# Loading the first head's keys as two halves in a long decode-attention kernel

## The chip, the cores and the metric

The kernel runs on one core of a Trainium2 chip. The metric is the device time of one execution in microseconds (us), of the slowest core, which here is the only one. "A 2% change" would be 27 us. A load is issued when SyncE hands it to the DMA queue, and it has landed when the last of its data are in the buffer.

## The reference

Two decode steps with one query token each, side by side. Part A has 32 heads with 32,768 keys each. Part B has 32 query heads on 8 key heads and a window of the last 4,096 keys.

```python
q = x @ wq                                   # 1 x 512 times 512 x 4096, then 32 heads of 128
scores = einsum(q, k_cache) * 128 ** -0.5    # A: 32 heads x 32768 keys; B: the last 4096 keys
p = softmax(scores)
out = einsum(p, v_cache).reshape(1, 4096) @ wo
return concatenate([A, B])
```

Each head of part A has 8 MB of keys and 8 MB of values (the MB of the load list, 2^20 bytes), and each byte is used once.

## The kernel before

Part B runs first, then a loop over the 32 heads of part A. The key buffer has three thirds of 4 MB. A head of A takes two of them, alternately (1, 0) and (1, 2). The value buffer holds one head of A. All loads are issued by SyncE, in order, into one queue; SyncE waits with each load until the buffer that it overwrites has been read.

```python
def load_k(self, g, parts):
    w = HALF * DH
    src = self.kv_src("k", "A", g)[:, 0, :]
    lo = min(self.k_thirds(g))
    free = [self.free["k"][t] for t in self.k_thirds(g)]
    if parts == 1:
        self.load(self.kbuf[:, w * lo:w * lo + 2 * w], src, self.mark("k", 0), *free)
        sem = self.mark("k", 1)
        self.op("sp", lambda e: e.sem_inc(sem, 16))
    else:
        for i, t in enumerate(self.k_thirds(g)):
            self.load(self.kbuf[:, w * t:w * t + w], src[:, w * (t - lo):w * (t - lo) + w], self.mark("k", i), *free)
# ...
for g in range(NQH):                       # NQH = 32
    self.loop = {"pe": g, "dve": g // 2}
    self.load_k(g, 1 if g < NQH - 1 else 2)   # the last head is split already
    self.load_v(g)
    self.emit_qcopy(g)
    self.emit_unit("A", g)     # TensorE transposes the keys (L560), VectorE copies (L564), TensorE: scores (L583)
    self.emit_stats("A", g)    # maximum and exponentials
    self.emit_PT("A", g)       # TensorE transposes the probabilities
    self.emit_PV("A", g)       # TensorE: probabilities times values (L663)
```

TensorE's program is one loop for all heads. It waits for semaphore `ksem0` before a head's first half and for `ksem1` before its second. With a single load, `ksem0` tells of the landing, and SyncE itself raises `ksem1`, so that the loop's waits are the same for both forms.

Of the kernel before, what the change touches and what calls it, by code (L numbers as in the profile page):

```python
# [10 lines left out]
NQH = 32  # L11
# [42 lines left out]
class _Kernel:  # L54
# [118 lines left out]
    def emit(self, eng):  # L173
# [22 lines left out]
        def body(e):  # L196
# [17 lines left out]
            for k, it in enumerate(need):  # L214
                cur, plan = {}, []
                for n in it:
                    w = []
                    for name, (sem, val) in n.items():
                        if name not in sems:
                            continue  # L220
                        rel = val - start[name] - step[name] * k
                        if rel > cur.get(name, 0):
                            cur[name] = rel
                            w.append((name, rel))
                    plan.append(sorted(w))
                plans.append(plan)
            for k, plan in enumerate(plans):
                for p, q in zip(plan, plans[-1]):
                    assert p == q or (k == 0 and set(p) <= set(q)), (eng, k, p, q)
# [126 lines left out]
# [5 lines that stand above are left out]
        if parts == 1:  # L361
            self.load(self.kbuf[:, w * lo:w * lo + 2 * w], src, self.mark("k", 0), *free)
            sem = self.mark("k", 1)
            self.op("sp", lambda e: e.sem_inc(sem, 16))
        else:
            for i, t in enumerate(self.k_thirds(g)):
                self.load(self.kbuf[:, w * t:w * t + w], src[:, w * (t - lo):w * (t - lo) + w], self.mark("k", i), *free)
# [26 lines left out]
    def plan(self):  # L394
        self.lsem = {"k": self.ksem, "v": self.vsem}
        self.fill = {w: [0, 0] for w in "kv"}
        self.free = {"k": [None] * 3, "v": [None] * 2}
        self.nbatch = 0
        self.copies = []
        self.pending = []  # L400
        self.psread = self.ptread = self.sread = self.accread = None
        self.gath = self.qcopy = self.hcopy = self.qread = None
        self.constants()
        a, b = self.X["A"], self.X["B"]

        self.load_wq("B")
        self.load_b("k", 0)
        self.load_wq("A")
        self.load_b("k", 1)
        self.emit_qproj("B")  # L410
        self.emit_unit("B", 0)
        self.emit_qproj("A")
        self.emit_stats("B", 0)
        self.emit_unit("B", 1, {1: lambda: self.emit_PT("B", 0)})
        self.emit_stats("B", 1)
        for g in range(2):
            if g == 1:
                self.emit_PT("B", g)
            self.load_b("v", g)
            self.emit_PV("B", g)  # L420
        self.emit_spread("B")

        for g in range(NQH):
            self.loop = {"pe": g, "dve": g // 2}
            self.load_k(g, 1 if g < NQH - 1 else 2)
            self.load_v(g)
            self.emit_qcopy(g)
            self.emit_unit("A", g)
            self.emit_stats("A", g)
            self.emit_PT("A", g)  # L430
            self.emit_PV("A", g)
        self.loop = {}
        for n in ("B", "A"):
            for part in range(len(self.WO_CUTS[n]) - 1):
                self.load_wo(n, part)
        for i in range(16):
            self.load(self.marks[0:i + 1, 16 * i:16 * i + 16], self.X["A"]["wo"][0:i + 1, 0:16], self.marksem[i])
        self.emit_spread("A")
        self.emit_proj()
        for i in range(16):  # L440
            self.op("sp", lambda e, i=i: e.wait_ge(self.marksem[i], 16))
        for n in ("B", "A"):
            self.op("sp", lambda e, n=n: e.wait_ge(self.outsem[n], 16))
# [336 lines left out]
```

## Time and profile before

The median of three runs was 1328.44 us (1326.69 to 1328.87).

| Reading | Value |
|---|---|
| Span of the profiled execution | 1326.1 us |
| Main DMA queue | 570 MB, 99.7% of 16 engines' span |
| TensorE, VectorE busy | 73%, 57% |
| One 8 MB load of keys or values, landing to landing | 19.35 us |
| TensorE waits for keys | 155.8 us in 30 waits |

These are lines from the page of the kernel before. Each character of the DMA row is the busy tenths of one fortieth of the span, and the GB/s row has the bytes of the same slices.

```profile
span 1326.1 us, 28802 instructions
...
PE 965.5 (73%) x13239; PEld 676.2 (51%) x13239; DVE 754.4 (57%) x1351; ACT 54.8 (4%) x167; POOL 2.2 (0%) x17
...
DMA  9999999999999999999999999999999999999998
...
q1 hardware_dynamic: 13048, 570.44, 99.7%
```

The DMA queue is the limit from the first slice to the last. The other engines have to be in time with buffers, no more. The Trainium skill's page "Perfetto Trace Analysis" says that with 16 DMA engines occupancy is misleading (section "Identifying the Most-Contended Engine"), and that the gaps on the limiting engine are what to look for (section "Optimization Strategy" below it). 99.7% doesn't show the one gap of this stream.

The timeline of the kernel before shows that gap's cause. The columns are start, duration, engine, line, operation and count; brackets give the idle time before it and what ended it.

```profile
start us, us, engine line op out<-in xcount [idle before <-releaser]
...
54.03 0.34 SPq L326 DMA_DIRECT2D kbuf<-in_A_k_cache_dram  x1
...
82.84 5.90 PE L560 MATMUL psT<-ident,kbuf 128*128 128x128 bf16 x64 [12.82 <-DMA kbuf<-in_A_k_cache_dram]
...
93.99 0.33 SPq L326 DMA_DIRECT2D kbuf<-in_A_k_cache_dram  x1
...
104.75 3.37 PE L560 MATMUL psT<-ident,kbuf 128*128 128x128 bf16 x31 [3.11 <-issue]
...
113.42 5.92 PE L663 MATMUL psACC<-vbuf,ptsb 128*4 128x512 bf16 x64 [0.69 <-ACT ptsb L638]
...
119.40 0.33 SPq L326 DMA_DIRECT2D vbuf<-in_A_v_cache_dram  x1
```

The keys of head 0 are issued at 54.03, and TensorE begins at 82.84. The keys of head 1 are issued at 93.99, when half of head 0's keys have been read. The values of head 1 can be issued only after head 0's last value matmul, at 119.40. The list of DMA issues, asked for the moments of the last two, ends with the time from issue to landing:

```profile
kbuf<-in_A_k_cache_dram SPq DMA_DIRECT2D x1, 27.5
...
vbuf<-in_A_v_cache_dram SPq DMA_DIRECT2D x1, 21.9
```

So head 1's keys landed at 93.99 + 27.5 = 121.5 us. The values were issued only 2.1 us before that, and they landed at 141.3. In the trace's landing records the two are 19.79 us apart, 0.44 more than the usual 19.35.

The list of waits has TensorE's total wait for keys (total, times, longest):

```profile
PE psT L560 <- DMA kbuf<-in_A_k_cache_dram: 155.8, 30, 12.8
```

The end of the chain that ended last (start, duration, what), with the last weights' landing and what TensorE and VectorE do after it:

```profile
1290.47 29.99 DMA kbuf<-in_A_wo_dram
...
1320.50 0.61 PE psT L742 x6
...
1321.14 0.70 DVE pb L745
...
1321.89 1.38 PE psPT L725 x18
...
1323.29 0.42 DVE out_sb L731
```

### The profile page before, as it was taken

Reading aid. Unit: us, or ns where it says so; the run is one execution under the profiler, and the core shown is the slowest. Engines: PE = TensorE matmul, PEld = TensorE weight load, DVE = VectorE, ACT = ScalarE, POOL = GpSimd, SP = SyncE. Lnnn points to the kernel's source line nnn. Section 1 sums busy time; section 2 is a strip of 40 time slices with the busy share of each in tenths; the row PEclk is TensorE's granted clock in tenths of the full one; section 3 lists DMA queues with packets and bytes.
Section 4 is the critical chain, followed back from the end, with each engine's and each line's share of the span. In section 5 each row is a group of like instructions: output and inputs, shape, how many; then the busy total and the mean of one; then the engine's idle time right before and its main releaser. Section 6 shows DMA issues by size and latency. Waiting matters only on the chain. (4 is left out here: it accounts for less than half of the span.)

```text
span 1326.1 us, 28802 instructions
## 1 busy us (share of the span) xinstructions
PE 965.5 (73%) x13239; PEld 676.2 (51%) x13239; DVE 754.4 (57%) x1351; ACT 54.8 (4%) x167; POOL 2.2 (0%) x17
## 2 busy tenths in 40 slices
PE   4657678776777878677787767778777767877786
PEld 3344446554444655444455544445554444555453
DVE  4555456665455666545566654556665455666563
ACT  0000000000000000000000000000000000000000
POOL 0000000000000000000000000000000000000000
PEclk9878798888789888878988887898887788888788
DMA  9999999999999999999999999999999999999998
GB/s 404 444 420 413 443 443 411 443 443 425 429 443 437 417 443 441 417 439 443 431 423 443 441 413 443 443 423 431 443 435 419 443 439 419 439 443 429 425 443 348
DMA packets 13348, 570.60 MB, mean 430 GB/s; under 512 B 1812, under 2 KB 1816, under 8 KB 2200
## 3 DMA queue, kind: packets, MB, share of 16 engines
q1 hardware_dynamic: 13048, 570.44, 99.7%
q8 instruction: 8, 0.13, 0.0%
q10 hardware_dynamic: 288, 0.00, 0.0%
q14 instruction: 4, 0.03, 0.0%
HBM read 570.43 MB, written 0.00 MB: 430 GB/s over the span
## 5 line engine op out<-in xcount | busy, mean ns | idle before, releaser
L564 DVE COPY kt<-psT 128x1024 bf16<-128x1024 bf16 x1056 | 656.0, 684 | 241.1 <-PE psT L560 239.4
L560 PE MATMUL psT<-ident,kbuf 128*128 128x128 bf16 x8448 | 582.3, 235 | 170.3 <-DMA kbuf<-in_A_k_cache_dram 155.8
L560 PEld LDWEIGHTS psT<-ident,kbuf 128*128 128x128 bf16 x8448 | 542.7, 106 | 262.5 <-DMA kbuf<-in_A_k_cache_dram 163.7
L663 PE MATMUL psACC<-vbuf,ptsb 128*4 128x512 bf16 (+1 forms) x2112 | 184.0, 524 | 23.0 <-ACT ptsb L638 22.0
L583 PE MATMUL psS<-kt,qw 128*32 128x512 bf16 x2048 | 157.6, 385 | 15.0 <-DVE kt L564 15.0
L677 DVE TENSOR_SCALAR oc_A<-psACC,hot_A 128x128 f32<-128x128 f32 x32 | 11.2, 351 | 248.5 <-PE psG L690 248.5
L663 PEld LDWEIGHTS psACC<-vbuf,ptsb 128*4 128x4 bf16 (+1 forms) x2112 | 59.7, 110 | 137.7 <-issue 88.7
L611 ACT ACTIVATE psb<-psS,nb_A 128x512 bf16<-128x512 f32 x32 | 22.0, 687 | 1171.0 <-DVE nb_A L610 1171.0
L583 PEld LDWEIGHTS psS<-kt,qw 128*32 128x32 bf16 x2048 | 34.0, 95 | 57.5 <-DVE kt L564 30.9
L690 PE MATMUL psG<-oc_A,hw 128*32 128x128 f32 (+1 forms) x128 | 19.3, 227 | 52.3 <-DVE oc_A L679 52.3
L690 PEld LDWEIGHTS psG<-oc_A,hw 128*32 128x32 f32 x128 | 11.4, 109 | 62.4 <-DVE oc_A L679 55.0
L635 PE MATMUL psPT<-ident,psb 128*128 128x128 bf16 x136 | 18.0, 275 | 34.0 <-ACT psb L611 34.0
L679 DVE SCALAR_TENSOR_TENSOR oc_A<-psACC,hot_A,oc_A 128x128 f32<-128x128 f32 x96 | 33.7, 351 | 3.4
L600 DVE TENSOR_REDUCE tr_in<-psS 128x1 f32<-128x512 f32 x34 | 23.5, 692 | 17.2 <-PE psS L583 17.2
L635 PEld LDWEIGHTS psPT<-ident,psb 128*128 128x128 bf16 x136 | 10.1, 117 | 37.1 <-ACT psb L611 36.7
L604 PE MATMUL psACC<-rows,tr_in 128*1 128x64 f32 x64 | 8.7, 217 | 25.6 <-DVE tr_in L600 25.6
L638 ACT ACTIVATE ptsb<-psPT 128x512 bf16<-128x512 bf16 x34 | 20.3, 597 | 29.9 <-PE psPT L635 29.9
L604 PEld LDWEIGHTS psACC<-rows,tr_in 128*1 128x1 f32 x64 | 2.7, 81 | 35.1 <-DVE tr_in L600 35.1
L608 PE MATMUL psACC<-mr_A,nscale 1*128 1x1 f32 x64 | 12.1, 256 | 9.7 <-DVE mr_A L607 9.7
L608 PEld LDWEIGHTS psACC<-mr_A,nscale 1*128 1x128 f32 x64 | 9.4, 182 | 15.7 <-DVE mr_A L607 15.7
L610 DVE COPY nb_A<-psACC 128x1 f32<-128x1 f32 x32 | 5.0, 158 | 15.0 <-PE psACC L608 15.0
L607 DVE TENSOR_REDUCE mr_A<-psACC 1x1 f32<-1x64 f32 x32 | 6.8, 213 | 11.7 <-PE psACC L604 11.7
(85 smaller groups left out, 73.0 us busy)
## 6 DMA issues: line engine op xcount, KB each, us to landing
kbuf<-in_B_k_cache_dram SPq DMA_DIRECT2D x2, 4096.0 KB, 31.8
vbuf<-in_B_v_cache_dram SPq DMA_DIRECT2D x2, 4096.0 KB, 25.4
kbuf<-in_A_k_cache_dram SPq DMA_DIRECT2D x2, 4096.0 KB, 23.1
vbuf<-in_B_wq_dram SPq DMA_DIRECT2D x1, 4096.0 KB, 12.4
vbuf<-in_A_wq_dram SPq DMA_DIRECT2D x1, 4096.0 KB, 32.0
kbuf<-in_B_wo_dram SPq DMA_DIRECT2D x2, 2048.0 KB, 33.1
kbuf<-in_A_wo_dram SPq DMA_DIRECT2D x1, 1408.0 KB, 26.3
kbuf<-in_A_wo_dram SPq DMA_DIRECT2D x1, 1024.0 KB, 28.6
```

The costliest lines, as they stand in the source:

```text
L560: inst = e.transpose(T[:, 128 * k:128 * k + 128], src[:, DH * k:DH * k + DH], self.ident[:, :])
L564: self.copies.append(self.op("dve", lambda v: v.tensor_copy(KT[:, :], T[:, :]), o, to="pe"))
L583: inst = e.matmul(self.S[32 * c:32 * c + 32, :], lhsT=win, rhs=self.kt[(bb + c // 2) % NKT][:, 512 * (c % 2):512 * (c % 2) + 512], start=b ...
L600: o = dve(lambda v: v.reduce_max(tr["in"][:, 0:1], self.S[:, :], axis=AXX), self.sdone, self.k_pool, to="pe" if name == "A" else None)
L604: o = self.op("pe", lambda e: e.matmul(self.ACC[0:1, 0:64], lhsT=tr["in"][:, 0:1], rhs=self.rows64[:, :], start=True, stop=True, skip_grou ...
L608: o = self.op("pe", lambda e: e.matmul(self.ACC[:, 64:65], lhsT=self.nscale[:, :], rhs=t["mr"][0:1, :], start=True, stop=True, skip_group_ ...
L611: self.sread = self.op("act", lambda s: s.activation(out=self.psb[:, :], in_=self.S[:, :], func=ACTF.Exp, bias=t["nb"][:, k:k + 1], scale= ...
L635: inst = e.transpose(PT[:, 128 * jj:128 * jj + 128], self.psb[:, 128 * jj:128 * jj + 128], self.ident[:, :])
L638: self.ptread = self.op("act", lambda s: s.activation(out=self.ptsb[:, :], in_=PT[:, 0:512], func=ACTF.Copy), self.psread, to="pe")
L663: inst = e.matmul(acc[32 * c:32 * c + rows, 0:512], lhsT=lhsT, rhs=rhs, start=begin, stop=end, tile_position=(0, 32 * c), skip_group_check ...
L679: o = self.op("dve", lambda v, src=src, hot=hot: v.scalar_tensor_tensor(out=oc, in0=src, scalar=hot, in1=oc, op0=ALU.mult, op1=ALU.add), p ...
L690: return self.op("pe", lambda e: e.matmul(self.G[0:32, c0 + c:c0 + c2], lhsT=win, rhs=t["oc"][g % len(t["oc"])][:, c:c2], start=False, sto ...
```

## The change

The intent: TensorE shall begin on the first head when half of its keys are there. The rest of the schedule then moves up.

```diff
@@ load_k
         if parts == 1:
             self.load(self.kbuf[:, w * lo:w * lo + 2 * w], src, self.mark("k", 0), *free)
             sem = self.mark("k", 1)
-            self.op("sp", lambda e: e.sem_inc(sem, 16))
+            self.op("sp", lambda e: e.sem_inc(sem, 16), self.free["k"][0] if g == 1 else None)
@@ plan
-            self.load_k(g, 1 if g < NQH - 1 else 2)
+            self.load_k(g, 1 if 0 < g < NQH - 1 else 2)
```

The first line is a guard. Head 0's second half now raises `ksem1` by landing. SyncE must not raise the same semaphore for head 1 until TensorE is through with that half.

## The prediction

> **What bounds the kernel now.** The DMA stream. The queue table of the profile gives the main queue 99.7% of sixteen engines' span, 570 MB at 430 GB/s; TensorE is busy 73% and VectorE 57%. The Trainium skill ("DMA: Bandwidth & Descriptors", "Where 436 GB/s comes from") puts the fabric ceiling at 435.2 GB/s. This trace agrees: spreading each DMA packet over its duration, I count 433 to 434 GB/s in mid-run. Steady-state 8 MB loads land 19.35 us apart. TensorE waits for keys in nearly every head (the wait list: 155.8 us in 30 waits), so an earlier TensorE is worth time only where the queue would otherwise run dry.
>
> **Where the queue does run dry.** Once, by the same count. Issue and landing times around the first two heads (timeline of SyncE, DMA list): keys of head 0 issued 54.03, landed 82.80; values of head 0 landed 102.15; keys of head 1 issued 93.99, landed 121.48; values of head 1 issued only at 119.40, because the value buffer is released by head 0's last value matmul (113.42 to about 119.3 in the timeline). Some engines have by then finished their share of the keys: from 119 to 124 us the count falls to 260 to 380 GB/s, a deficit of about 0.56 MB, 1.3 us of full rate. But the engines that idled were the ones ahead; the last engine sets the landing. The values of head 1 land at 141.27, 19.79 us after the keys, against 19.35 normally: 0.44 us lost. Later loads are issued well ahead.
>
> **What the change does.** Head 0's keys are two loads of 4 MB. The first should land about 9.7 us earlier than the whole did (the last head is already split so, and its halves take 9.72 and 9.71 us) at about 73.2, and TensorE starts there instead of at 82.84. The first half's transposes took 11.2 us, so the second half has landed at 82.9 when they end at about 84.3: no new wait. Scores end at about 99.7, softmax and its transposes take 4.1 us, and the value matmuls run from about 103.8 (values landed 102.2) to 109.7. So head 1's keys are issued at about 84.3 instead of 93.99, head 1's values at about 109.8 instead of 119.40, 9 us before the queue would run out: no hole.
>
> Costs: one more DMA issue on SyncE (0.33 to 0.43 us, queue full: hidden); halves cost 19.43 against 19.35 us, 0.08 us. SyncE's semaphore increment for head 1 now waits until TensorE has read head 0's second half; the following value load waits for a later matmul anyway, so this is free. That wait is necessary: the skill (same page, "Why a DMA increments its semaphore by 16 and not by 1") warns that two increments in flight on one semaphore can satisfy a wait too early; no run here shows it.
>
> From head 2 on the landings only shift by the recovered 0.44 us. Net gain about 0.4 us (1.3 if every idle engine counted), 0.03%, below the spread of the runs (1326.69 to 1328.87).
>
> **Predicted:** 1328.0 us, range 1326.2 to 1329.4. Faster by over 2%: 1%; within 2%: 98.5%; slower by over 2%: 0.5%.
>
> **What would show it.** Right: TensorE's wait for head 0's keys (12.82 us) falls to about 3; head 1's values issued near 110; no fall of the DMA rate at 119 to 124; values of head 1 land 19.35 us after its keys; later periods unchanged at 19.35. Wrong: head 1's keys or values not issued earlier, a longer period, or slower halves.
>
> **What would make it wrong.** A new stall of SyncE, slower half rows, or a longer first-pass stall of TensorE (3.1 us at 101.6).

## The result

The changed kernel's median was 1328.07 us (1326.90 to 1328.94, 6 runs); the kernel before had 1328.65 (1326.69 to 1329.37, 6 runs). The ratio is 0.9998, with a 95% interval of 0.9985 to 1.0011: the same. Ratios here are the mean time of one kernel's fast runs over that of the other's of the same rounds, so not quite the ratio of the medians.

From the page of the changed kernel:

```profile
span 1327.2 us, 28802 instructions
...
q1 hardware_dynamic: 13192, 570.44, 99.6%
```

The profiled execution is 1.1 us longer than the one of before, although its gap is gone. The timeline of the changed kernel:

```profile
54.76 0.82 SPq L326 DMA_DIRECT2D kbuf<-in_A_k_cache_dram  x2
...
73.18 6.23 PE L560 MATMUL psT<-ident,kbuf 128*128 128x128 bf16 x64 [2.67 <-DMA kbuf<-in_A_k_cache_dram]
...
84.66 0.33 SPq L326 DMA_DIRECT2D kbuf<-in_A_k_cache_dram  x1
...
95.25 3.31 PE L560 MATMUL psT<-ident,kbuf 128*128 128x128 bf16 x31 [2.94 <-issue]
...
103.86 6.21 PE L663 MATMUL psACC<-vbuf,ptsb 128*4 128x512 bf16 x64 [0.69 <-ACT ptsb L638]
...
110.13 0.33 SPq L326 DMA_DIRECT2D vbuf<-in_A_v_cache_dram  x1
```

TensorE starts 9.66 us earlier. Head 1's keys and values are issued 9.3 us earlier each. The issue-to-landing times of those two in the list of DMA issues:

```profile
kbuf<-in_A_k_cache_dram SPq DMA_DIRECT2D x1, 36.9
...
vbuf<-in_A_v_cache_dram SPq DMA_DIRECT2D x1, 30.8
```

The keys were issued 9.3 us earlier and took 9.4 us longer: they land at 121.6, as before. The values land at 140.9 us instead of 141.3. An earlier issue into a queue that is still full only waits longer in it.

TensorE's waits for keys sum to 152.4 us, only 3.4 less than before. Head 0's wait fell from 12.8 to 2.7 us, but head 1 has a new one of 9.5 us (the second line, from the timeline); in the kernel before TensorE came to head 1's keys as they landed. The early start is paid back at the next load. SyncE also has a new wait, the guard (the second fence is SyncE's own list):

```profile
PE psT L560 <- DMA kbuf<-in_A_k_cache_dram: 152.4, 31, 9.5
...
121.61 0.61 PE L560 MATMUL psT<-ident,kbuf 128*128 128x128 bf16 x4 [9.47 <-DMA kbuf<-in_A_k_cache_dram]
```

```profile
SPq L364 <- PE psS L583: 14.1, 1, 14.1
```

The end of the chain that ended last in the changed kernel:

```profile
1288.23 32.18 DMA kbuf<-in_A_wo_dram
...
1320.45 1.03 PE psT L742 x6
...
1321.51 0.70 DVE pb L745
...
1322.25 2.53 PE psPT L725 x18
...
1324.80 0.42 DVE out_sb L731
```

Here is where the 1.1 us came from. The third part of the last weights, for which these 6 matmuls wait, lands as before, at 1320.4, but the same 6 and 18 matmuls take 1.03 and 2.53 us instead of 0.61 and 1.38. The last result is 1.5 us later; what follows it took 0.4 us less. The granted clock is the share of its full clock that TensorE is allowed to run at. The table by stretches gives the stretch, its length, the busy time (and count) of PE, PEld, DVE, ACT and POOL, the granted clock of TensorE, the DMA share and the GB/s. First the kernel before, then the changed one:

```profile
1320.00:1322.00 2.00, 0.71 (x8) 0.19 (x10) 0.69 (x1) 0.00 (x0) 0.00 (x0) 1.00 0.82 304
1322.00:1324.00 2.00, 1.25 (x18) 0.56 (x14) 0.42 (x1) 0.00 (x0) 0.00 (x0) 1.00 0.03 3
```

```profile
1320.00:1322.00 2.00, 1.02 (x6) 0.10 (x6) 0.49 (x1) 0.00 (x0) 0.00 (x0) 0.50 0.42 149
1322.00:1324.00 2.00, 1.75 (x14) 0.85 (x16) 0.20 (x1) 0.00 (x0) 0.00 (x0) 0.50 0.01 0
```

The clock was full in one execution and half in the other. The first question is then which differences belong to the kernel and which to one execution.

### The profile page after: what moved, and what is told of

It reads as the page before. It is cut to its first block, busy times and chain, and to the rows that moved or that the text cites. A ratio compares the mean times of both kernels' runs of the same rounds, so it can differ in the third digit from the quotient of the medians.

```text
span 1327.2 us, 28802 instructions
## 1 busy us (share of the span) xinstructions
PE 970.6 (73%) x13239; PEld 677.0 (51%) x13239; DVE 753.9 (57%) x1351; ACT 54.8 (4%) x167; POOL 2.2 (0%) x17
## 5 line engine op out<-in xcount | busy, mean ns | idle before, releaser
L560 PE MATMUL psT<-ident,kbuf 128*128 128x128 bf16 x8448 | 581.4, 235 | 165.4 <-DMA kbuf<-in_A_k_cache_dram 152.4
L663 PE MATMUL psACC<-vbuf,ptsb 128*4 128x512 bf16 (+1 forms) x2112 | 187.6, 532 | 22.8 <-ACT ptsb L638 22.0
L600 DVE TENSOR_REDUCE tr_in<-psS 128x1 f32<-128x512 f32 x34 | 23.5, 692 | 17.1 <-PE psS L583 17.1
```

The source lines that it names most:

```text
L560: inst = e.transpose(T[:, 128 * k:128 * k + 128], src[:, DH * k:DH * k + DH], self.ident[:, :])
L600: o = dve(lambda v: v.reduce_max(tr["in"][:, 0:1], self.S[:, :], axis=AXX), self.sdone, self.k_pool, to="pe" if name == "A" else None)
L663: inst = e.matmul(acc[32 * c:32 * c + rows, 0:512], lhsT=lhsT, rhs=rhs, start=begin, stop=end, tile_position=(0, 32 * c), skip_group_check ...
```

## The experiments

Twelve runs were made. Three measures, taken from the trace's records, compare them.

- The *stream*: from the landing of part B's last values to the landing of the last head's values. All of A's loads lie in it; the start and the end of the kernel don't.
- *Mean stream*: the same between the means of the two loads' landing records. Each load leaves 16 of them, and it has landed with the last.
- *Missing*: the shortfall of the bytes moved against 434 GB/s, in us at that rate, from 117 to 127 us. Each packet's bytes are spread evenly over its duration.

| Run | Head 1's values issued | Landed after head 1's keys | Missing | Stream | Mean stream |
|---|---|---|---|---|---|
| before, first profile | 119.40 | 19.79 | 1.29 | 1239.30 | 1240.20 |
| e1, before again | 117.57 | 19.34 | 0.22 | 1238.52 | 1239.24 |
| e12, before, third | 117.91 | 19.34 | 0.45 | 1238.53 | 1239.50 |
| e8, before, dummies at the end | 118.17 | 20.70 | 0.97 | 1239.93 | 1239.93 |
| e9, before, dummies at head 0 | 113.67 | 19.35 | 0.01 | 1238.67 | 1239.16 |
| changed, first profile | 110.13 | 19.35 | 0.01 | 1238.63 | 1239.23 |
| e2, changed again | 108.93 | 19.35 | 0.01 | 1238.60 | 1239.22 |
| e3, second half loaded first | 116.73 | 19.35 | 0.06 | 1238.62 | 1239.24 |
| e10, increment later | 108.41 | 19.35 | 0.01 | 1238.61 | 1239.21 |
| e7, e11, changed, dummies at the end | 108.63, 110.16 | 19.36, 19.35 | 0.01 | 1238.60, 1238.62 | 1239.21, 1239.22 |
| e5, values issued after a tag | 122.13 | 22.31 | 3.75 | 1241.89 | 1242.79 |

The last landing record and the mean don't tell the same. In the first profile the gap delayed the early records more than the late ones: those of head 1's keys span 2.06 us, those of its values 0.66. So the loss is 1.07 us on the mean, and the last record shows only 0.44 of it. In e8 it is the other way round: the span grew from 1.88 to 2.37 us, the mean lost 0.77 us, and the last record 1.35. On the mean, the loss between head 1's keys and values follows the moment of the issue: 0.00 us for an issue 5.0 us before the keys' landing (e3), 0.10 for 4.2 (e1), 0.32 for 3.7 (e12), 0.77 for 3.3 (e8), 1.07 for 2.1 (the first profile), and 3.60 for 0.2 after it (e5). It also stays: the mean streams of e12, e8, the first profile and e5 are 0.28, 0.71, 0.98 and 3.57 us above the 1239.22 of the changed kernel.

**Theories.** Mine: the queue of loads sets the time, and an earlier TensorE is worth only the time for which the queue would be dry. The main rival: TensorE's waits for keys are on the path, so that an earlier start shortens the run. Smaller rivals: two loads help by themselves; the guard costs something; the gap is an accident of one execution.

### e1 and e12: the kernel before, twice more

No edit.

> The kernel before, unchanged, for a second profile. If the hole belongs to the kernel and not to one execution: head 1's values are issued within 1 us of 119.4, the DMA rate falls between 119 and 124 us, and the values land 19.6 to 19.9 us after head 1's keys. If it was an accident: 19.35 us and no fall. For the end of the run: the time from the last landing that TensorE waits for to its last result should be near 2.9 us where the granted clock there is 1.0, and near 4.4 us where it is 0.5.

> The kernel before for a third profile of its own. Head 1's values issued between 117 and 120 us; if after 118, 0.4 to 1.4 us more than 19.35 between the landings of head 1's keys and values; if before, nothing lost.

The kernel before has the gap in some executions only. In e1 the values were issued at 117.57 us and nothing was lost in the landing. This is the timeline of e1:

```profile
95.00 0.33 SPq L326 DMA_DIRECT2D kbuf<-in_A_k_cache_dram  x1
...
112.21 5.32 PE L663 MATMUL psACC<-vbuf,ptsb 128*4 128x512 bf16 x64 [0.69 <-ACT ptsb L638]
...
117.57 0.33 SPq L326 DMA_DIRECT2D vbuf<-in_A_v_cache_dram  x1
```

Of the two readings that my expectation offered, "within 1 us of 119.4" fell, and "an accident" held in the landing. e12 held: issued at 117.91, nothing lost in the landing, though 0.45 us of the engines' time was missing (0.28 us on the mean stream). The issue follows the end of the value matmuls, and their start and length vary with the granted clock: 5.92, 5.32 and 5.78 us in the three profiles.

The clock records show the state changing between 0.5 and 1.0 after multiples of 3.4 us. The skill's page "TensorE: Matmul & The Clock Gate" (Part 1, "The HAM clock gate") describes this: the clock is halved after an idle window of about 3.4 us, and the windows run freely, so that the moment of the change differs from run to run. This trace agrees on the windows, with stretches of 3.4, 6.8, 17.1 and 27.3 us. That a whole window has to be idle it doesn't show: in the first profile TensorE stopped at 101.64 us and the clock fell at 104.46, 2.8 us later. The page also says that the clock comes back after about 3.4 us of sustained work; here it came 2.6 to 6.0 us after TensorE began on head 0's keys at half clock (e2, e1).

### e2: the changed kernel again

No edit.

> The changed kernel, unchanged, for a second profile and a tighter ratio. Theory (the stream of loads sets the time, one hole of 0.44 us is closed): ratio 0.9995 to 1.0000, head 1's values issued near 110 us, landing 19.35 us after head 1's keys. Rival (an earlier TensorE shortens the run by itself): up to 9.7 us less, ratio 0.993.

The ratio was 0.9996 (0.9982 to 1.0009), and the values were issued at 108.93 us. In no profile with an early start and an unhindered issue was the queue dry: the values land 19.35 or 19.36 us after the keys in all five of them. The rival of a shorter run by 9.7 us is excluded by the interval.

### e3: the same two loads in the other order

```diff
-            for i, t in enumerate(self.k_thirds(g)):
+            for i, t in list(enumerate(self.k_thirds(g)))[::-1 if g == 0 else 1]:
```

> The two loads of head 0 in the other order: the half that TensorE needs first is loaded last, so it can't begin early; all else is as in the changed kernel. Theory (only the early start of TensorE closes the hole): TensorE starts on head 0 near 82.9 us, head 1's values are issued near 119.4, the hole is back, they land 19.7 to 19.9 us after head 1's keys, and the split's own 0.07 us stays. Rival (two loads instead of one close it by themselves): issued near 110 and no hole. Time within 0.1% of both in either case.

The timeline of e3:

```profile
55.50 0.81 SPq L326 DMA_DIRECT2D kbuf<-in_A_k_cache_dram  x2
...
83.10 5.57 PE L560 MATMUL psT<-ident,kbuf 128*128 128x128 bf16 x64 [11.82 <-DMA kbuf<-in_A_k_cache_dram]
...
116.73 0.33 SPq L326 DMA_DIRECT2D vbuf<-in_A_v_cache_dram  x1
```

TensorE began at 83.10, as expected, and the issue went back from 110 to 116.7: the split alone doesn't move it, the early start does. But my expectation that the gap would come back missed. 116.73 is still early enough, so the run doesn't decide about the gap itself. The ratio was 1.0003 (0.9988 to 1.0018).

### e4: all heads split

```diff
-                self.load(..., self.mark("k", i), *free)
+                self.load(..., self.mark("k", i), *free,
+                          self.free["k"][self.k_thirds(g - 1)[1]] if i and g else None)
...
-            self.load_k(g, 1 if 0 < g < NQH - 1 else 2)
+            self.load_k(g, 2)
```

The added dependency is the change's guard for every head. By my reading, a build without it has a race: two increments could meet the same wait for `ksem1`. This is what the skill's page "DMA: Bandwidth & Descriptors" ("Why a DMA increments its semaphore by 16 and not by 1") warns of; no run here shows the fault on the chip.

> Every head's keys in two halves. Theory (the queue is never dry after head 1, and a split costs 0.07 us): TensorE starts each head's keys 9.7 us earlier, nothing is gained, and 30 more splits cost about 2.1 us: ratio 1.0005 to 1.0025. Rival (waits of TensorE for keys are on the path): tens of us less, since those waits sum to 152 us.

The ratio was 1.0015 (1.0001 to 1.0028), median 1330.86 us (1330.21 to 1330.90). The stream is 1241.03 us, 2.41 more than the mean of the changed kernel's two profiles, for 30 more splits: 0.08 us each. The waits of TensorE are the instructive part:

```profile
PE psACC L664 <- DMA vbuf<-in_A_v_cache_dram: 129.3, 31, 5.2
...
PE psT L561 <- DMA kbuf<-in_A_k_cache_dram: 51.5, 25, 2.7
```

The 152.4 us of waits for keys have shrunk to 51.5. In their place TensorE waits 129.3 us for values. When TensorE is the faster partner, an earlier start only moves its wait to the next load. A hundred microseconds less of waits for keys made the run longer, not shorter: the main rival has fallen.

### e5: values issued when the queue is surely dry

```diff
+            if g == 1:
+                self.load(self.tag[:, :], self.X["A"]["wo"][0:16, 0:16], self.tagsem)
+                self.free["v"] = [*self.free["v"], (self.tagsem, 16)]
             self.load_v(g)
+            self.free["v"] = self.free["v"][:2]
```

The cut leaves out the lines that make the tag's buffer and its semaphore.

> The changed kernel, but SyncE issues head 1's values only when a tiny load behind head 1's keys has landed, so only when the queue has surely run dry. Theory (a late issue costs what the queue is idle after it ran dry): issue near 121.9 us, [...]values land 21 to 22.5 us after head 1's keys, every later landing 2 to 3 us later, ratio 1.0010 to 1.0025. Together with the issues seen at 110 (nothing lost), 116.7 and 117.6 (nothing lost) and 119.4 (0.44 us lost) it gives the threshold. Rival (the time of that issue doesn't matter): no later landing.

Issued at 122.13 us, landed 22.31 after the keys, stream 3.27 us longer than the changed kernel's (mean of its two profiles), ratio 1.0025 (1.0009 to 1.0040): as the theory has it, though the later landings slip by a little more than the expected 2 to 3 us. The first packets of the values began 0.96 us after the issue. An issue that comes after the queue has run dry costs about 3 us on this path, and it isn't made up by the 60 or so loads that follow.

### e6: values issued after the next head's keys

The edit holds head 1's value load back and issues it after `load_k(2)`.

```diff
-            self.load_v(g)
+            if g == 1:
+                held = self.mark("v", 0), self.free["v"][:]
+            else:
+                if g == 2:
+                    self.load(self.vbuf[:, :], self.kv_src("v", "A", 1)[:, 0, :], held[0], *held[1])
+                self.load_v(g)
```

> The changed kernel, but head 1's values are issued after head 2's keys. Theory: nothing is issued until TensorE has read the first half of head 1's keys, near 132 us, so the queue is dry from about 120 to 134, and again later while head 1's values are late: 12 to 24 us lost in all, equal within 1 us to the DMA time that is missing in the trace; ratio 1.009 to 1.018. Rival (one hole of that kind is made up by later slack): under 3 us lost.

The ratio was 1.0160 (1.0144 to 1.0175), median 1349.28 us. The table by stretches of e6, with the same columns:

```profile
118.00:124.00 6.00, 2.40 (x23) 2.40 (x24) 1.17 (x2) 0.00 (x0) 0.00 (x0) 0.50 0.23 98
124.00:130.00 6.00, 6.00 (x98) 4.94 (x96) 5.84 (x11) 0.00 (x0) 0.00 (x0) 0.95 0.00 0
130.00:136.00 6.00, 6.00 (x104) 4.95 (x102) 6.00 (x11) 0.00 (x0) 0.00 (x0) 1.00 0.54 186
...
172.00:178.00 6.00, 4.80 (x66) 1.94 (x66) 0.00 (x0) 0.00 (x0) 0.00 (x0) 0.68 0.00 0
```

The queue is dry twice, although TensorE is busy the whole time from 124 to 136. Counted from 117 to 200 us, 21.17 us of DMA time are missing; the stream is 21.14 us longer than the changed kernel's. This is the cleanest evidence for the theory: a long dry time of the queue is lost one for one, and nothing later gives it back. The short gaps in the table bear this out only roughly: 0.45, 0.97, 1.29 and 3.75 us missing went with mean streams longer by 0.28, 0.71, 0.98 and 3.57 us.

### e9: the gap closed without a split

```diff
         self.emit_spread("B")
+        self.keep_warm(44)    # 44 dummy matmuls 128 x 128 x 512 while TensorE waits for head 0's keys
```

> The kernel before (head 0's keys in one load) with 44 dummy matmuls in TensorE's wait for those keys. Theory (whether the queue runs dry depends on when head 0's last value matmul ends, and that on the granted clock of TensorE since the keys landed): clock 1.0 at 82.8 us, so head 0's first half takes about 9.8 us instead of 11.2, head 1's values are issued between 114.5 and 117.5 us, the queue isn't dry, they land 19.35 us after the keys, and from the last early value load to the last head's values the time is 1238.5 us, as in the changed kernel or 0.08 less, without a split. Rival (only the split closes the hole): issued at 118 or later and over 0.3 us lost. Time within 0.1% of before.

The timeline of e9:

```profile
70.56 11.36 PE L741 MATMUL psT<-ptsb,ident 128*128 128x512 bf16 x44
...
83.22 3.82 PE L561 MATMUL psT<-ident,kbuf 128*128 128x128 bf16 x64 [1.30 <-DMA kbuf<-in_A_k_cache_dram]
...
113.67 0.33 SPq L326 DMA_DIRECT2D vbuf<-in_A_v_cache_dram  x1
```

The first 64 transposes took 3.82 us instead of 5.90, and the values were issued at 113.67 us, even earlier than I expected. The values land 19.35 us after the keys. So TensorE's pace on head 0 decides whether the kernel before has its gap, and the split is one of two ways to be clear of it. The clock isn't all of that pace in e9: a stop of TensorE in the middle of head 0's keys (told at the end of the next section) took 0.77 us here and 3.11 in the first profile, perhaps because the dummies move the later instructions. With the longer stop, an estimate from these numbers puts the issue at 116.0 us, still early enough. The ratio was 1.0001 (0.9986 to 1.0016). The stream was 1238.67 us, 0.15 more than in e1; on the mean it is 0.08 less than in e1 and 0.06 less than in the changed kernel, near the cost of a split.

### e10: the increment without the wait

```diff
-            self.load_k(g, 1 if 0 < g < NQH - 1 else 2)
+            late = self.load_k(g, 1 if 0 < g < NQH - 1 else 2)   # for g == 1 returns the semaphore
             self.load_v(g)
+            if late is not None:
+                self.op("sp", lambda e, late=late: e.sem_inc(late, 16))
```

> The changed kernel, but SyncE's increment for head 1 comes after the issue of head 1's values, so it needs no wait of its own. Theory (that wait costs nothing): head 1's values issued between 108.5 and 110.5 us as before, landing 19.35 us after its keys, head 2's keys issued near 133. Rival (the new wait delays SyncE's issues): head 1's values issued earlier by over 1 us.

The 14.1 us wait is gone from SyncE's list. Head 1's values were issued at 108.41 us, next to 108.93 and 108.63 of executions that have the wait (e2, e7). Against the first profile of the changed kernel that is 1.7 us earlier, but TensorE's value matmuls ended earlier by as much: they began at 103.65 and took 4.71 us, against 103.86 and 6.21. In both the issue comes 0.05 to 0.06 us after their end. (The expected 108.5 was missed by 0.09.) The guard costs nothing that these profiles show.

### e7, e8 and e11: TensorE kept busy at the end

```diff
             for part in range(cut):
+                if name == "A":
+                    self.keep_warm((5, 7, 5)[part])      # e11: (1, 6, 5)
                 o = self.proj_part(...)
             strips = ...
+            self.keep_warm(3)
```

e7 and e11 are the changed kernel with this edit, e8 is the kernel before with that of e7.

> The changed kernel with dummy matmuls in TensorE's waits for the last weights; no load changes. Theory (the spread of 2 us from run to run is the granted clock of TensorE after the last loads): clock 1.0 there in every run, 3.0 to 3.5 us from the third part of the last weights to the last result instead of up to 4.8, the runs within 1 us of each other, ratio 0.9990 to 0.9997. Rival (the spread comes from the loads): the spread stays at 2 us.

> The kernel before with the same dummy matmuls. Theory: as the changed kernel with them within 0.5 us, its runs as close together; then the change itself is worth between -0.1 and +0.4 us, seen with the clock's spread taken away. If the change is worth more, this one is slower by that.

> The changed kernel with fewer dummy matmuls at the end (1, 6, 5 before the three parts and 3 before the last sum, where the first try had 5, 7, 5 and 3), so that they are over before each part of the last weights lands. Theory: 3.2 to 3.4 us from the landing of the third part to the last result instead of 4.0, clock 1.0, ratio to the kernel before 0.9988 to 0.9995. If the dummies aren't enough, clock 0.5 and up to 4.8 us.

From the landing of the third part of the last weights to the last result, it took 3.25 us where the clock was 1.0 (before, e3, e5, e6), 4.82 where it was 0.5 (changed, e1, e4, e9, e10, e12; e1's expectation had 2.9 and 4.4, both too low), and 4.14 once, with a mean clock of 0.71 (e2). With the dummies the clock was 1.0 in all three profiles. It took 3.97 us in e7, because the dummies were still running when the weights came, 3.37 in e8, and 3.26 in e11. These are the last steps of e11's chain:

```profile
1320.22 0.60 PE psT L754 x6
...
1321.61 1.38 PE psPT L725 x18
```

So the clock moves the end by 1.6 us. But the expected narrower spread missed: the runs span 2.03 us in e7, 2.81 in e8 and 1.85 in e11. The ratios were 0.9993 (0.9980 to 1.0007), 1.0005 (0.9991 to 1.0018) and 0.9999 (0.9985 to 1.0012); the expected 0.9988 to 0.9995 of e11 missed too. So did e8's: it was to be within 0.5 us of e7, and its median is 1.37 us above (1328.47 against 1327.10). By that expectation the change would be worth more than 0.4 us; but these are five runs each, the two ranges overlap, and e8's profile had a gap, so it stays open.

A part of what is left is the landing of the last weights: their third part landed 17.55 to 18.35 us after the last values. On the mean of the 16 landing records it is 17.61 or 17.62 us in all 14 profiles, so the difference lies in how far the records are apart: those of the third part span 1.03 us in the first profile, which had the gap, and 2.52 in the changed kernel's first. The rest stays open. No version is shown to beat the others.

## Why the prediction was right

**The limit and the size.** It said that the DMA stream is the limit and that about 0.4 us is to be had. e4 shows that TensorE's waits aren't on the path. e5 and e6 show that dry time of the queue is lost for good. The measured medians, 1328.07 and 1328.65 us, agree with it, but differences that small are far inside the interval. What carries the statement is the stream: 1238.60 to 1238.63 us in the five profiles with an early start, and 1238.52, 1238.53, 1239.30 and 1239.93 in four of the kernel before (on the mean, 1239.21 to 1239.23 against 1239.24, 1239.50, 1240.20 and 1239.93).

**The steps.** Predicted against measured in the changed kernel: TensorE starts at 73.2 (73.18), its wait falls to about 3 us (2.67), head 1's keys are issued at 84.3 (84.66), scores end at 99.7 (the maximum starts at 99.80), the values are issued at 109.8 (110.13) and land 19.35 us after the keys (19.35). The cost of a split was predicted as 0.08 us; e4 gives 0.08. The guard was predicted to be free; e10 agrees.

**What was off.** Three points, all below the noise of the time.

- "0.44 us lost" was read from one execution and taken for a property of the kernel. Over the four profiles of the kernel before (e8 among them, whose edit comes only at the end) the keys-to-values interval lost 0.44, 0, 0 and 1.35 us: on average 0.45, but by luck of the clock. Issues at 117.91 us or earlier lost nothing in the landing, those at 118.17 and later did. In an execution without the gap the change costs its 0.08 us. The prediction also let only the last engine count. On the mean of the landing records the first profile lost 1.07 us, nearer to the 1.3 that it gave for the case that "every idle engine counted".
- "From head 2 on the landings only shift by the recovered 0.44 us": between the two first profiles the shift is 0.31 us at head 2's keys (160.58 to 160.27), and 0.68 at the last values (1302.74 to 1302.06). The loads after the gap took 0.33 us longer on the last record; on the mean they took the same (1161.25 and 1161.28 us), so it is again the records moving apart.
- The sum ended with the stream. Behind it the granted clock adds 0 to 1.6 us, more than the gain. It made the changed kernel's profiled execution the longer one, although its last values landed 0.68 us earlier. Of these 0.68 us only 0.05 were left at the landing of the weights' third part, whose records lay further apart than before.

Not tested: the 3 us for which TensorE stands in the middle of head 0's keys with no wait that the profile shows (3.11 us before, 2.94 changed, in head 0 only). Without it, an estimate from these numbers puts the issue of the kernel before at 116.3 us, clear of the gap. The traces do show something at that moment: in each of the 14 profiles a packet of 16,384 bytes in the queue that the profile lists as "q8 instruction" ended 1.3 to 1.6 us before TensorE went on (before: packet from 102.22 to 103.24, TensorE again at 104.75; changed: 92.80 to 93.82, and 95.25). This fits a wait for instructions, but other such packets came without a long stop, and no run tests it.

## What to carry to other kernels

When one queue is the limit, ask of every wait elsewhere only whether it makes the queue run dry: find the issue that comes last relative to the end of the load ahead of it, and take the loss from the interval between landings, not from the idle engine. Take it from all landing records of a load, since the last one alone can show less or more than was lost. An earlier start of a faster engine is paid back as a longer wait for its next load. For an effect below the spread of the runs, profile each kernel more than once, since a gap of one execution can be the luck of a clock.

## What the Trainium skill lacked or had wrong

- "DMA: Bandwidth & Descriptors": it has no cost for splitting a large load in a queue that stays full. Here two 4 MB loads instead of one of 8 MB, back to back in a full queue, cost 0.08 us.
- The same page gives a fabric ceiling of 435.2 GB/s ("Where 436 GB/s comes from") and says in the note beside it that for loads from HBM a limit of about 358 GB/s per core binds. Here one core alone, with the rest of the chip not used by this program, moved 433 to 434 GB/s in mid-run: the ceiling is what held. (The page's own table of measured loads and the page "HBM Reference", section "Specifications (TRN2)", are nearer: about 425 GB/s for a core that streams alone.)
- "DMA: Bandwidth & Descriptors" doesn't say how late a load may be issued before the queue runs dry. Here an issue 5.0 us before the load ahead had landed lost nothing; one 4.2, 3.7, 3.3 and 2.1 us before it lost 0.10, 0.32, 0.77 and 1.07 us on the mean of the landing records.
- "TensorE: Matmul & The Clock Gate": it puts the release of the clock at around 4 us of sustained work, with 0.5 us either way. Here it came 2.6 to 6.0 us after TensorE began.
- No page gives a length for the stop of TensorE in the first pass of its loop (2.1 to 3.7 us in 13 profiles, 0.8 in e9). If it is a wait for instructions, it belongs to "Runtime: NRT & Kernel Launch".
